# First block and second row of x issued from other queues, and the opening's VectorE order changed, in a fused Fourier-mixing and gated-MLP layer

## The chip, the cores and the metric

The kernel runs on one core of one Trainium2 chip. The metric is the device time of one execution in microseconds (us). Before the change the median of three runs is 931.79 us (931.69 to 931.9). One further execution was recorded by the hardware profiler: it took 932.1 us, of which the traced span of the core is 930.0 us.

The engines are TensorE (PE for matmuls, PEld for its weight loads), VectorE (DVE), ScalarE (ACT), GpSimd (POOL) and SyncE (SP). SyncE does nothing here but issue DMAs; ScalarE can issue DMAs too, from its own instruction stream.

## The reference

The layer has an input x of 2048 rows of 512 numbers (S = 2048, D = 512) and a condition row c that gives six modulation rows through `silu(c) @ w_mod`.

```
h = layernorm(x) * (1 + ca) + sa
a, b = h @ dft_hid_re.T, h @ dft_hid_im.T
y = dft_seq_re @ a - dft_seq_im @ b          # 2048 x 2048 matrices
x = x + ga * y
h = layernorm(x) * (1 + cb) + sb
z = gelu(h @ w_in);  z1, z2 = halves of z;  z2 = layernorm(z2)
out = x + gb * ((z1 * (w_sp @ z2 + b_sp)) @ w_out)
```

Everything is float32. A product is computed as three matmuls of rounded parts: a number is split into a high part (rounded to the matmul's format) and a low part (the rest), and high times high, high times low and low times high are added.

## The kernel before, in words

The first stage multiplies the transposed sequence matrices with the normalised rows of x. It goes in steps n = 0, 1, 2, ...; step n takes one group of 128 rows of x, numbered s = n at the start, and one 128x512 tile of the sequence matrix. `mm_a(n)` issues the step's matmuls on TensorE. From step 4 on a step is 12 matmuls (four column blocks by three products, L97 to L99), in the order high x high, high x low, low x high inside each column block. Steps 1 to 3 are also 12 matmuls each (L576), but in three groups of four: first high of x with high of the matrix (`hh`, `ah`), then `hh` with the low part `al`, then the low part of x, `hl`, with `ah`. Step 0 is different: it multiplies the unsplit tiles in float32 (L570), so that it needs no split.

What a step needs is made by the other engines:

- The matrix arrives in blocks of 512x512, loaded by SyncE into a tile `stage` (two buffers). A block serves four steps, k = 0 to 3. For the first blocks `load_pairs` (L168) loads it in two halves, h = 0 and h = 1, each in four parts of 128 KB (32 partitions each); half 0 serves k = 0 and 1, half 1 serves k = 2 and 3. `turn_dft` transposes one tile on VectorE (L174 where k < 2, L177 else). `prep_hi(n)` does this transposition into `t` and then has ScalarE make the high part `ah` (L289). `prep_lo(n)` makes the low part `al` on VectorE (L307).
- x's rows come by `load_x`: "row" 0 and "row" 1 of the first group of four (64 KB parts, four each, L453), then rows 2 and 3 in one DMA of 512 KB (L448). `stats_first(s)` makes mean and variance of one such row on VectorE (three instructions: L467, L472, L473) and hands them to GpSimd, which makes the factors (L474, L475). `whole_first(0)` normalises row 0 on ScalarE (L484). `hi_first(s)` makes the high part `hh` straight from x on ScalarE (L510, and a one-column instruction L512), `norm_x(s)` the normalised row `xn` on ScalarE (L121), and `lo_h(s)` the low part `hl` = `xn` - `hh` on VectorE (L552). `split_first(0)` and `rest_first(0)` make row 0's two parts for later use, on ScalarE (L494) and GpSimd (L498).

The order on each engine is the order in which these calls are written: the opening, step by step by hand, stands at the end of the listing, and after it the loop over n calls `prep(n)` (which is `prep_hi(n + 3)` and `prep_lo(n + 2)`, where not yet done), `mm_a(n)` and further work that is bound to n. An engine works through its own list in order; an instruction that waits holds up all behind it on the same engine. The program gives its DMAs eight completion semaphores in turn: a DMA that takes up a semaphore is not issued before the DMA that had it last has landed, so that at most eight are under way. Before the opening, `keep_busy` runs three matmuls on a constant tile (L389).

The first DMAs of the program are issued by SyncE and ScalarE together: `two` names the issuing engine of each of four parts. ScalarE's first own work, an activation-table load for the silu function, stands behind its DMA issues (L1121).

Of the kernel before, what the change touches and what calls it, by code (L numbers as in the profile page):

```python
# [20 lines left out]
def fnet_gmlp_kernel(  # L21
# [32 lines left out]
    nc = tc.nc  # L54
# [81 lines left out]
    src, SRC_G = [], []  # L136
# [14 lines left out]
    stage, T, AH, AL = {}, {}, {}, {}  # L151
# [12 lines left out]
    def load_pairs(tile_, a, h, engs=(nc.sync,) * 4, bs=slice(0, 16)):  # L164

        v = a.rearrange("(b j) (h a s) -> h a j b s", j=32, a=4, h=2)
        for q in range(4):
            engs[q].dma_start(tile_[32 * q:32 * q + 32, bs, 64 * h:64 * h + 64], v[h, q][:, bs, :])  # L168

    def turn_dft(n, block, k, bs=slice(0, 16)):  # L170

        t = T[n].rearrange("p (b i) -> p b i", i=32)
        if SRC_G[n // 4] or k < 2:
            nc.vector.transpose(t[:, bs, :], block[:, bs, 32 * k:32 * k + 32])  # L174
        else:
            v = block.rearrange("p b (h i c) -> p b h i c", h=2, c=2)
            nc.vector.transpose(t[:, bs, :], v[:, bs, 1, :, k - 2])  # L177
# [3 lines left out]
    def load(b):  # L181
        if b < len(src):
            stage[b] = blocks.tile([P, 16, P], F32, tag="stage", bufs=2, name=f"stage{b}")
            if SRC_G[b]:
                load_block(stage[b], src[b])
            else:
                for h in range(2):
                    load_pairs(stage[b], src[b], h)
        elif b < len(src) + 2:
            j = b - len(src)  # L190
            XB.append(blocks.tile([P, 4, Q], F32, tag="stage", bufs=2, name=f"xb{j}"))
            for g in range(2):
                nc.sync.dma_start(XB[j][:, 2 * g:2 * g + 2], ht_d[g].rearrange("(k p) t -> p k t", p=P)[:, 2 * j:2 * j + 2])
                for kk in range(2):
                    TT[2 * j + kk, g] = XB[j][:, 2 * g + kk]
        elif 4 * (b - NB0) < NE - N4:
            i, gh = divmod(b - NB0, NQ)
            g, h = divmod(gh, 2)
            p = PROD[i]
            stage[b] = blocks.tile([P, 2, 16, 64], F32, tag="stage", bufs=2, name=f"stage{b}")  # L200
            for r in range(2):
                load_half(stage[b][:, r], s_d[S_OF[p], r, g] if p in S_OF else
                          quad(w_sp, r + (2 if p == 4 else 0), g + (2 if p == 1 else 0)), h)
# [5 lines left out]
    def squares(dst, block, k):  # L209
        nc.vector.transpose(dst.rearrange("p (b i) -> p b i", i=32), block[:, :, 32 * k:32 * k + 32])  # L210
# [10 lines left out]
    def slot(i, name, dtype=F32):  # L221
        return slots[0].tile([P, Q], dtype, tag=f"slot{i}", bufs=1, name=name)
# [19 lines left out]
    def form_t(n):  # L242

        if n < N1:
            gg, p, kk = (n - N2) // 4, (n - N2) // 2 % 2, n % 2
            return TT[2 * p + kk, gg]
        p = YPROD[(n - N1) // 4 % len(YPROD)]
        gg, kk = divmod(n % 4, 2)
        a, b, c, d = TT[kk, gg], TT[2 + kk, gg], TT[kk, 2 + gg], TT[2 + kk, 2 + gg]
        return {6: S2[gg, kk], 7: a if n < N3 else c, 4: b if n < N3 else d, 5: c if n < N3 else a, 3: d if n < N3 else b}[p]  # L250
# [21 lines left out]
    def prep_hi(n):  # L272
        if n >= NE or n in highs:
            return
        highs.add(n)
        if N2 <= n < N4:
            T[n] = form_t(n)
        else:
            b, k = divmod(n, 4) if n < N2 else (NB0 + (n - N4) // 4, (n - N4) % 4)
            if b != NB0:  # L280
                T[n] = blocks.tile([P, Q], F32, tag="t", bufs=2, name=f"t{n}")
            if b == NB0:
                assert n in T
            elif n >= N4:
                squares(T[n], stage[b][:, k % 2], k // 2)
            else:
                turn_dft(n, stage[b], k)
        AH[n] = SE[2][:, n - N4] if N4 <= n < N4 + 4 else blocks.tile([P, Q], F32R, tag="ah", bufs=4, name=f"ah{n}")
        nc.scalar.activation(AH[n], T[n], AF.Copy)  # L289
        if not N2 <= n < N4 and k == 3:  # L290
            stage.pop(b)
            if b != NB0:
                load(b + 2)


    def prep_lo(n):
        if n >= NE or n in lows:
            return
        lows.add(n)
        if N2 <= n < N4 and n % 4 == 3:  # L300
            AL[n] = slot(0, f"al{n}", F32R) if slots else zrow[0].tile([P, Q], F32R, tag="z1u", bufs=6, name=f"al{n}")
        elif N4 <= n < N4 + 4:
            AL[n] = slot(9 + n - N4, f"al{n}", F32R)
        else:
            AL[n] = blocks.tile([P, Q], F32R, tag="al", bufs=3, name=f"al{n}")
        t = T.pop(n)
        nc.vector.tensor_tensor(AL[n], t, AH[n].bitcast(F32), op=ALU.subtract)  # L307
# [134 lines left out]
    def load_x(g, ks=range(4), engs=(nc.sync,) * 4):  # L442

        if g not in XG:
            XG[g] = spool.tile([P, 4, D], F32, tag="x", bufs=2, name=f"x{g}")
        k0, k1 = ks[0], ks[-1] + 1
        if not g and k0 == 2:
            nc.sync.dma_start(XG[g][:, 2:, :], x[2 * P:Q, :].rearrange("(p k) d -> p k d", k=2))  # L448
        else:
            v = (x.rearrange("(g a k i) d -> g a i k d", g=NQ, a=4, i=32)[g] if g else  # L450
                 x[:2 * P, :].rearrange("(a k i) d -> a i k d", a=4, i=32))
            for a in range(4):
                engs[a].dma_start(XG[g][32 * a:32 * a + 32, k0:k1, :], v[a][:, k0:k1, :])  # L453
        for k in ks:
            X[4 * g + k] = XG[g][:, k, :]
# [4 lines left out]
    def stats_first(s):  # L460

        sums_first(s)
        norm_first(s)

    def sums_first(s):
        M1[s] = spool.tile([P, 12], F32, tag="first", bufs=4, name=f"first{s}")
        nc.vector.bn_stats(M1[s][:, :6], X[s])  # L467

    def norm_first(s):

        mv = M1[s][:, 8:]
        nc.vector.bn_aggr(mv[:, :2], M1[s][:, :6])  # L472
        nc.vector.tensor_scalar(mv[:, 1:2], mv[:, 1:2], EPS, None, op0=ALU.add)  # L473
        nc.gpsimd.tensor_tensor(mv[:, 2:3], mv[:, 1:2], mhalf, op=ALU.pow)  # L474
        nc.gpsimd.tensor_scalar(mv[:, 3:4], mv[:, 0:1], mv[:, 2:3], -1.0, op0=ALU.mult, op1=ALU.mult)  # L475
        NRM[s] = mv[:, 2:3], mv[:, 3:4]
# [22 lines left out]

    def turn_whole(n):  # L500
        T[n] = blocks.tile([P, Q], F32, tag="t", bufs=2, name=f"t{n}")
        for bs in PARTS:
            turn_dft(n, stage[0], n, bs)
        highs.add(n)
        lows.add(n)

    def hi_first(s):
        h_hi[s] = hpool.tile([P, ND, P], F32R, name=f"hh{s}")
        h = h_hi[s].rearrange("p k (a i) -> p k a i", i=32)
        nc.scalar.activation(h, X[s].rearrange("p (a k i) -> p k a i", a=4, i=32), AF.Identity,  # L510
                             bias=NRM[s][1], scale=NRM[s][0])
        nc.scalar.activation(h_hi[s][:, 0, :1], ones[:, :1], AF.Copy)  # L512
# [16 lines left out]
    def ones_x(s):  # L529
        LN[s] = spool.tile([P, D], F32, tag="xn", bufs=4, name=f"xn{s}")  # L530
        nc.gpsimd.memset(LN[s][:, 0:1], 1.0)

    def norm_x(s):

        if s not in LN:
            ones_x(s)
        elif s > 3:
            nc.gpsimd.memset(LN[s][:, 0:1], 1.0)
        apply(LN[s][:, 1:], X.pop(s)[:, 1:], NRM.pop(s))
# [9 lines left out]
    def lo_h(s):  # L549
        h_lo[s] = hpool.tile([P, ND, P], F32R, name=f"hl{s}")  # L550
        lo, h = parts_h(s, h_lo)
        nc.vector.tensor_tensor(lo, h, parts_h(s, h_hi)[0].bitcast(F32), op=ALU.subtract)  # L552
        LN.pop(s)
# [557 lines left out]
            mm([n])  # L1111


    PARTS = (slice(0, 16),)
    two = (nc.sync, nc.sync, nc.scalar, nc.scalar)
    load_x(0, range(1), two)
    stage[0] = blocks.tile([P, 16, P], F32, tag="stage", bufs=2, name="stage0")
    for bs in PARTS:
        load_pairs(stage[0], src[0], 0, two, bs)
    load_x(0, range(1, 2), two)  # L1120
    nc.scalar.activation(sc, ones[:, :ND], AF.Silu)  # L1121
    load_x(0, range(2, 4))
    load_pairs(stage[0], src[0], 1)
# [9 lines left out]
    stats_first(1)  # L1133
    prep_hi(1)
    hi_first(1)
    prep_lo(1)
    stats_first(2)
    norm_x(1)
    stats_first(3)
    hi_first(2)  # L1140
    lo_h(1)
    prep_hi(2)
    norm_x(2)
    prep_hi(3)
    prep_lo(2)
    lo_h(2)
    hi_first(3)
    norm_x(3)
    prep_lo(3)
    split_first(0)  # L1150
# [36 lines left out]
    for j, turn, weigh, row, fold, hi in ((0, (25, 26, 27, 28), (29, 29, 30, 30), 26, (34, 34, 35, 36), (40, 37, 38, 39)),  # L1187
# [8 lines left out]
        n = weigh[3] + 1  # L1196
# [20 lines left out]
    for t in range(NQ):  # L1217
        n = 8 * NQ * (t + 1)
# [136 lines left out]
    for i, p in enumerate(PROD):  # L1355
        for k in range(8):
            n = NB[p] + 2 * k
# [11 lines left out]
    for f in range(NF):  # L1369
        n = N4 + 24 + 8 * f  # L1370
# [109 lines left out]
```

## Time and profile before

| | before |
|---|---|
| median of 3 runs | 931.79 us |
| the profiled execution | 932.1 us |
| its span | 930.0 us |
| PE busy | 923.3 us, 99% of the span, 4053 matmuls |
| DVE busy | 737.4 us, 79%, 1217 instructions |
| ACT busy | 409.0 us, 44% |
| POOL busy | 198.9 us, 21% |
| chain that ended last | PE 98%, DVE 1%, DMA 0%, ACT 0% |
| DMA | 157.88 MB, mean 170 GB/s |

"Busy" is the time in which an engine worked on instructions; "chain that ended last" follows the work back from the last instruction, at each step to what released it. In the timeline a row gives the start in us from the span's start, the time that it took in us, the engine (SPq and ACTq are DMA issues from SyncE's and ScalarE's instruction streams), the line of the kernel, the operation, out<-in with shapes, and how often it was merged (x2); in square brackets, where there is one, the idle time of the engine before it and what ended that.

### The profile page before, as it was taken

The numbers are of one execution on the slowest core, as the hardware profiler recorded it, in microseconds if no ns is written. First come the engines' busy times: TensorE is split into PE (matmuls) and PEld (weight loads), VectorE is DVE, ScalarE is ACT, GpSimd is POOL, SyncE is SP. The second block draws the span as 40 slices with busy tenths as digits, with TensorE's granted clock in tenths as the row PEclk, the third lists the DMA queues.
The fourth block names the chain that finished last, engine by engine and source line by source line (L and its number), as shares of the span: only waits on it lengthen the run. The fifth ranks groups of instructions, "written<-read, shape, count | busy, mean of one in ns | idle before, by whom it ended". The sixth has DMA issues, their size and how long they took to land.

```text
span 930.0 us, 12378 instructions
## 1 busy us (share of the span) xinstructions
PE 923.3 (99%) x4053; PEld 760.2 (82%) x4053; DVE 737.4 (79%) x1217; ACT 409.0 (44%) x734; POOL 198.9 (21%) x376
## 2 busy tenths in 40 slices
PE   8999999999999999999999999999999999999998
PEld 5888888888888888888888888888888888888887
DVE  6799968787687677875678788899799789886762
ACT  5694424232132222322577877674544544331121
POOL 2330000224554165323512321331000000000000
PEclk9999999999999999999999999999999999999999
DMA  9995762757539987996463764444464555744651
GB/s 222 225 226 116 142 158 46 193 148 173 156 88 294 281 255 215 276 341 229 140 217 131 277 201 103 123 102 104 104 146 103 130 141 140 176 102 149 184 179 57
DMA packets 261584, 157.88 MB, mean 170 GB/s; under 512 B 169456, under 2 KB 229104, under 8 KB 261392
## 3 DMA queue, kind: packets, MB, share of 16 engines
q1 hardware_dynamic: 247856, 119.58, 52.2%
q0 software_dynamic: 12272, 36.86, 11.4%
q10 hardware_dynamic: 1392, 0.66, 0.2%
q8 instruction: 32, 0.52, 0.2%
q14 instruction: 32, 0.26, 0.1%
HBM read 120.33 MB, written 36.71 MB: 169 GB/s over the span
## 4 chain that ended last, share of the span: by engine, by line
PE 98%; DVE 1%; DMA 0%; ACTq 0%; ACT 0%; issue 0%; DVEq 0%
PE gp L98 12%; PE gp L97 12%; PE gp L99 12%; PE gw L99 10%; PE gw L98 10%; PE gw L97 10%; PE yp L98 3%; PE yp L97 3%; PE yp L99 3%; PE op L98 3%; PE op L99 3%; PE op L97 3%; PE fp L98 1%; PE fp L97 1%; PE fp L99 1%; PE z2s L99 1%
## 5 line engine op out<-in xcount | busy, mean ns | idle before, releaser
L289 ACT ACTIVATE ah<-t 128x512 fp32r<-128x512 f32 x235 | 148.5, 632 | 363.3 <-DVE t L174 157.8
L307 DVE TENSOR_TENSOR al<-t,ah 128x512 fp32r<-128x512 f32 x235 | 160.4, 682 | 55.2 <-PE gp L98 31.4
L98 PE MATMUL gp<-al,hh 128*128 128x512 f32 x496 | 193.2, 390 | 0.0
L97 PE MATMUL gp<-ah,hh 128*128 128x512 f32 x496 | 193.2, 389 | 0.0
L99 PE MATMUL gp<-ah,hl 128*128 128x512 f32 x496 | 193.2, 389 | 0.0
L98 PE MATMUL gw<-al,bh 128*128 128x512 f32 x400 | 155.8, 389 | 0.0
L99 PE MATMUL gw<-ah,bl 128*128 128x512 f32 x384 | 149.7, 390 | 0.0
L97 PE MATMUL gw<-ah,bh 128*128 128x512 f32 x384 | 149.6, 389 | 0.0
L97 PEld LDWEIGHTS gp<-ah,hh 128*128 128x128 f32 x496 | 93.1, 188 | 19.5
L98 PEld LDWEIGHTS gp<-al,hh 128*128 128x128 f32 x496 | 93.1, 188 | 19.5 <-DVE al L307 0.2
L99 PEld LDWEIGHTS gp<-ah,hl 128*128 128x128 f32 x496 | 93.1, 188 | 19.2
L98 PEld LDWEIGHTS gw<-al,bh 128*128 128x128 f32 x400 | 75.1, 188 | 15.7
L97 PEld LDWEIGHTS gw<-ah,bh 128*128 128x128 f32 x384 | 72.1, 188 | 15.1
L99 PEld LDWEIGHTS gw<-ah,bl 128*128 128x128 f32 x384 | 72.1, 188 | 15.1 <-DVE bl L975 0.3
L174 DVE STREAM_TRANSPOSE t<-stage 128x512 f32<-128x512 f32 x112 | 78.2, 699 | 5.7 <-DMA stage<-in_A_dft_seq_re_dram 3.7
L210 DVE STREAM_TRANSPOSE t<-stage 128x512 f32<-128x512 f32 x108 | 76.2, 706 | 2.5 <-DMA stage<-in_B_w_sp_dram 1.5
L947 POOL DMA_DIRECT2D s_d<-sj x64 | 35.1, 548 | 112.1 <-DVE sj L939 86.5
L97 PE MATMUL yp<-hth,gh 128*128 128x512 f32 x128 | 49.9, 389 | 0.0
L98 PE MATMUL yp<-htl,gh 128*128 128x512 f32 x128 | 49.8, 389 | 0.0
L99 PE MATMUL yp<-hth,gl 128*128 128x512 f32 x128 | 49.8, 389 | 0.0
L692 POOL DMA_DIRECT2D ht_d<-hturn x62 | 40.9, 665 | 21.2 <-DVE hturn L688 17.4
L97 PE MATMUL op<-woh,uh 128*128 128x512 f32 x110 | 42.8, 390 | 0.0
(248 smaller groups left out, 1502.6 us busy)
## 6 DMA issues: line engine op xcount, KB each, us to landing
sj<-in_B_w_sp_dram SPq DMA_DIRECT2D x32, 512.0 KB, 7.1
s_d<-sj POOLq DMA_DIRECT2D x64, 256.0 KB, 4.4
stage<-s_d SPq DMA_DIRECT2D x128, 128.0 KB, 2.8
stage<-in_A_dft_seq_re_dram SPq DMA_DIRECT2D x48, 256.0 KB, 5.4
stage<-in_A_dft_seq_im_dram SPq DMA_DIRECT2D x48, 256.0 KB, 5.5
stage<-in_B_w_sp_dram SPq DMA_DIRECT2D x88, 128.0 KB, 3.2
stage<-in_A_dft_seq_im_dram SPq DMA_DIRECT2D x32, 128.0 KB, 3.7
wm<-in_w_mod_dram SPq DMA_DIRECT2D x16, 256.0 KB, 5.4
```

The source lines that it names most:

```text
L97: nc.tensor.matmul(acc, ah, bh, start=first, stop=False, skip_group_check=go_on)
L98: nc.tensor.matmul(acc, ah, bl, start=False, stop=False, skip_group_check=go_on)
L99: nc.tensor.matmul(acc, al, bh, start=False, stop=last, skip_group_check=go_on)
L174: nc.vector.transpose(t[:, bs, :], block[:, bs, 32 * k:32 * k + 32])
L210: nc.vector.transpose(dst.rearrange("p (b i) -> p b i", i=32), block[:, :, 32 * k:32 * k + 32])
L289: nc.scalar.activation(AH[n], T[n], AF.Copy)
L307: nc.vector.tensor_tensor(AL[n], t, AH[n].bitcast(F32), op=ALU.subtract)
L692: eng.dma_start(v[a, i], ht[32 * a:32 * a + 32].rearrange("c (b r) -> c b r", r=32))
L947: nc.gpsimd.dma_start(s_d[m, r, g][b * P:(b + 1) * P, :], a)
```

## The change

Three edits, all in the opening.

The loads: of the four parts of the first half block, three instead of two are issued by SyncE, and one instead of two by ScalarE. All four parts of x's row 1 are issued by SyncE, where two were issued by ScalarE. The order in which the DMAs are written stays: row 0, half 0 of block 0, row 1, rows 2 and 3, half 1 of block 0.

VectorE's order: the statistics of row 2 stand ahead of `al` of step 1 instead of behind it; `hl` of row 1 stands behind the transposition of step 2 and ahead of the statistics of row 3 (it stood behind these, and ahead of the transposition); the statistics of row 3 stand behind `hl` of row 1; `al` of step 2 stands ahead of the transposition of step 3. The order of ScalarE's and GpSimd's computing stays as it is.

The list `PARTS`, which had one slice over the whole tile, goes; the same instruction is made without it.

```diff
     def turn_whole(n):
         T[n] = blocks.tile([P, Q], F32, tag="t", bufs=2, name=f"t{n}")
-        for bs in PARTS:
-            turn_dft(n, stage[0], n, bs)
+        turn_dft(n, stage[0], n)
         highs.add(n)
...
-    PARTS = (slice(0, 16),)
     two = (nc.sync, nc.sync, nc.scalar, nc.scalar)
     load_x(0, range(1), two)
     stage[0] = blocks.tile([P, 16, P], F32, tag="stage", bufs=2, name="stage0")
-    for bs in PARTS:
-        load_pairs(stage[0], src[0], 0, two, bs)
-    load_x(0, range(1, 2), two)
+    load_pairs(stage[0], src[0], 0, (nc.sync, nc.sync, nc.sync, nc.scalar))
+    load_x(0, range(1, 2))
     nc.scalar.activation(sc, ones[:, :ND], AF.Silu)
     load_x(0, range(2, 4))
     load_pairs(stage[0], src[0], 1)
@@ -1133,18 +1130,18 @@
     stats_first(1)
     prep_hi(1)
     hi_first(1)
+    stats_first(2)
     prep_lo(1)
-    stats_first(2)
     norm_x(1)
+    hi_first(2)
+    prep_hi(2)
+    lo_h(1)
     stats_first(3)
-    hi_first(2)
-    lo_h(1)
-    prep_hi(2)
     norm_x(2)
+    prep_lo(2)
     prep_hi(3)
-    prep_lo(2)
+    hi_first(3)
     lo_h(2)
-    hi_first(3)
     norm_x(3)
     prep_lo(3)
     split_first(0)
```

## Rows read from the trace of the kernel before

**Rows 1.** Busy time by stretch: from:to, us, then PE, PEld, DVE, ACT, POOL busy (instructions).

```profile
7.06:14.15 7.09, 6.71 (x20) 3.62 (x20) 6.07 (x15) 4.14 (x9) 2.84 (x6) 1.00 1.09 255
...
19.73:60.00 40.27, 40.27 (x179) 33.30 (x178) 34.39 (x61) 28.05 (x57) 13.79 (x44) 1.00 1.19 225
60.00:920.00 860.00, 860.00 (x3794) 711.69 (x3793) 688.67 (x1129) 369.01 (x657) 179.54 (x314) 1.00 0.61 167
```

**Rows 2.** Chain that ended last, 0 to 20 us: start, us, what.

```profile
2.12 3.92 DMA stage<-in_A_dft_seq_re_dram
6.24 0.70 DVE t L174
...
14.15 5.73 PE gp L576 x24
```

**Rows 3.** Timeline of the first 30 us: DMA issues of SyncE.

```profile
1.65 0.95 SPq L168 DMA_DIRECT2D stage<-in_A_dft_seq_re_dram  x2
...
2.95 0.78 SPq L453 DMA_DIRECT2D x<-in_A_x_dram  x2
...
5.20 0.35 SPq L448 DMA_DIRECT2D x<-in_A_x_dram  x1
...
5.60 2.02 SPq L168 DMA_DIRECT2D stage<-in_A_dft_seq_re_dram  x4
```

**Rows 4.** Waits of SyncE, 0 to 40 us: total, times, longest.

```profile
SPq L448 <- DMA stage<-in_A_dft_seq_re_dram: 1.4, 1, 1.4
```

**Rows 5.** DMA issues at 7.1 to 7.2 us: count, size, us to landing.

```profile
stage<-in_A_dft_seq_re_dram SPq DMA_DIRECT2D x1, 128.0 KB, 4.1
```

**Rows 6.** DMA issues at 5.1 to 5.3 us.

```profile
x<-in_A_x_dram SPq DMA_DIRECT2D x1, 512.0 KB, 3.9
```

**Rows 7.** DMA issues at 2.9 to 3.0 us.

```profile
x<-in_A_x_dram SPq DMA_DIRECT2D x1, 64.0 KB, 3.3
```

**Rows 8.** DMA packets, both queues at work, 3.6 to 5.4 us.

```profile
DMA packets 1668, 0.48 MB, mean 265 GB/s; under 512 B 1631, under 2 KB 1631, under 8 KB 1668
```

**Rows 9.** DMA packets, SyncE's queue alone, 8.4 to 9.8 us.

```profile
DMA packets 1598, 0.40 MB, mean 284 GB/s; under 512 B 1598, under 2 KB 1598, under 8 KB 1598
```

**Rows 10.** Timeline of the first 30 us: VectorE.

```profile
9.49 0.69 DVE L307 TENSOR_TENSOR al<-t,ah 128x512 fp32r<-128x512 f32 x1 [0.70 <-ACT ah L289]
...
10.10 0.69 DVE L467 BATCH_NORM_STATS2 first<-x 128x6 f32<-128x512 f32 x1
...
11.11 0.69 DVE L467 BATCH_NORM_STATS2 first<-x 128x6 f32<-128x512 f32 x1
...
12.12 0.69 DVE L552 TENSOR_TENSOR hl<-xn,hh 128x512 fp32r<-128x512 f32 x1
...
12.73 1.30 DVE L177 STREAM_TRANSPOSE t<-stage 128x512 f32<-128x512 f32 x2
...
14.13 0.69 DVE L307 TENSOR_TENSOR al<-t,ah 128x512 fp32r<-128x512 f32 x1
...
17.08 0.69 DVE L552 TENSOR_TENSOR hl<-xn,hh 128x512 fp32r<-128x512 f32 x1 [0.87 <-ACT xn L121]
...
19.09 0.69 DVE L307 TENSOR_TENSOR al<-t,ah 128x512 fp32r<-128x512 f32 x1
```

**Rows 11.** Timeline of the first 30 us: ScalarE.

```profile
5.93 1.09 ACT L484 ACTIVATE xn<-x,first 128x256 f32<-128x256 f32 x2 [0.47 <-POOL first L475]
...
14.71 0.62 ACT L289 ACTIVATE ah<-t 128x512 fp32r<-128x512 f32 x1
...
16.18 0.80 ACT L121 ACTIVATE xn<-x,first 128x511 f32<-128x511 f32 x1
```

**Rows 12.** Timeline of the first 30 us: TensorE, weight loads and matmuls.

```profile
12.87 1.20 PE L576 MATMUL gp<-ah,hl 128*128 128x512 f32 x4 [0.26 <-DVE hl L552]
...
19.84 0.19 PEld L98 LDWEIGHTS gp<-al,hh 128*128 128x128 f32 x1
...
19.96 0.39 PE L98 MATMUL gp<-al,hh 128*128 128x512 f32 x1
```

## The prediction

> **What bounds the kernel now.** I began with the page's shares (PE busy 99% of the span), so the only time to be had is where TensorE stands still. Busy time by stretch shows where: from 19.73 us to 60 and from 60 to 920 the PE is busy for the whole stretch, to the hundredth [rows 1]. Whatever happens in the opening, the end therefore moves by as much as TensorE's place in its own list moves once it has run into that closed stretch, and by nothing else. The second view is the chain of waits of the first 20 us. It goes from the DMA of the first half block, issued by ScalarE at 2.12 and landed at 6.04, to the first transposition at 6.24 (0.20 after the landing), and by VectorE and ScalarE to matmuls that run without a break from 14.15 on [rows 2]. From 7.06 to 14.15 the PE was busy for 6.71 of 7.09 us [rows 1]; its one stated wait there is 0.26 for `hl` of row 1, ahead of the matmuls at 12.87 [rows 12].
>
> The third view, the engines' timelines, shows a point that the chain hides, since it had no idle time: step 4. Its second product needs `al`, which VectorE began at 19.09 and had after 0.69, at 19.78 [rows 10]; the weight load that goes with it is at 19.84 and its matmul at 19.96 [rows 12]. So `al` of step 4 came just in time, with no slack. An earlier PE before it gains nothing unless this `al` is earlier too, and if this `al` is later, the end is later. So I follow the change to that point.
>
> **The chain to that `al`, before.** ScalarE makes `ah` of step 3 at 14.71, then `hh` of row 3, then `xn` of row 3 at 16.18, which is done at 16.98 [rows 11]. VectorE has idled 0.87 for it and starts `hl` of row 3 at 17.08; two transpositions follow, then `ah` of step 4, then `al` at 19.09 [rows 10]. From `ah` of step 3 to this `al` are 19.09 - 14.71 = 4.38 us. None of these instructions is moved among its neighbours, so I carry the 4.38 over. What moves is the transposition of step 3, on which `ah` of step 3 waits: it is the second of the pair at 12.73 and ends at 14.03 [rows 10].
>
> **VectorE's new order.** The steps from instruction to instruction, from the same rows: a statistics group 1.01 (10.10 to 11.11 to 12.12), a subtraction 0.61 (9.49 to 10.10; 12.12 to 12.73), a transposition 0.60 (two take 1.30, one alone 0.70 [rows 2, 10]).
>
> - Statistics of row 2, now first. VectorE is free at 9.49 - 0.70 = 8.79 and idled until 9.49 for `ah` of step 1 [rows 10]. The edit puts 1.01 of work into this hole. But rows 2 and 3 of x, issued at 5.20 with 3.9 to landing, come at 9.1 [rows 3, 6]; 0.20 later, at 9.3, the statistics can begin. So the hole is not filled, it is kept for 0.5. `al` of step 1 starts at 9.3 + 1.0 = 10.3 and is done at 11.0. Behind this wait are queued `al` and the transposition of step 2, and TensorE's second group of step 1 waits for the former; that group starts near 11.5 (the third group at 12.87, less its wait of 0.26, less 1.1 for four matmuls, of which the third group shows 1.20 [rows 12]), so 11.0 is in time by about 0.4.
> - The transposition of step 2, now ahead of `hl` and of the statistics of row 3. VectorE is free for it at 10.3 + 0.6 = 10.9. It needs the second half of block 0, in four parts issued from 5.60 to 7.62 [rows 3]; the last goes out at about 7.13 and lands 4.1 later, at 11.2 [rows 5]. So it starts at 11.4, where it started at 12.73. In the order of before this landing was hidden by 1.5 us; now it decides.
> - From there: `hl` of row 1 at 12.0 (12.12 before), statistics of row 3 at 12.6, `al` of step 2 at 13.65, transposition of step 3 at 14.25, done at 14.95. Before, that was done at 14.03. Between the two transpositions now stand a statistics group and two subtractions, 2.2 us, where nothing stood.
> - `ah` of step 3 can start at about 15.0. Before, it was at 14.71, because ScalarE was still at `xn` of row 2, so only 0.3 of the 0.9 counts. ScalarE idles more than a microsecond ahead of it.
> - `al` of step 4: 15.0 + 4.38 = 19.4, done at 20.1. TensorE's matmul with it comes at 20.25 instead of 19.96: **+0.3**.
>
> **What TensorE gains, and loses again.** `ah` of step 2 follows a transposition that ends at 12.1, so step 2 no longer waits for it: `hl` of row 1 is done at 12.7, the third group of step 1 runs from 12.8 to 13.8, and step 2 starts there instead of at 14.15 (the 14.15 of [rows 2]). The 0.3 of gain is kept through steps 2 and 3 and ends at step 4 as a longer wait for `al` (0.3 + 0.3). Sum: 0 from the gain, +0.3 from `al`.
>
> **The queues.** SyncE issues at 0.47 each for parts of the block (0.95 for two) and 0.4 for parts of a row [rows 3]. Its list gets one part of the block and two of row 1 more: 0.47 + 0.8 = 1.3 us. These go into the 1.4 us in which it stood before the load of rows 2 and 3 and waited for a landing of the first half block [rows 4]; it is free at about 4.95 and that load still goes at 5.20. If the cover were gone by the landing being earlier, the load would go out up to 0.25 sooner, which helps. The cost of having three parts in one queue is not in the trace: from both sides, the half block lands between 0.3 sooner (no part of row 1 runs beside its last part in the other queue) and 0.5 later (the third part goes out 0.5 later). Row 1's last part goes out near 4.55 where it went at 3.5; by the 3.3 that a part of it took [rows 7] it lands at 7.85 at worst, at about 6.9 if bytes moved set it; I take the latter, since the bytes ahead of it are the same. Neither end reaches the sum: row 1's statistics at 8.0 would put the transposition of step 1 at 9.0, ahead of the 9.3 above, and step 2's transposition still waits for 11.2. At the first matmul nothing is gained either: it waits for row 0 normalised at 5.93, which itself stood 0.47 for GpSimd's factors [rows 11], so that ScalarE's freedom from three DMA issues stays idle.
>
> The Trainium skill ("DMA: Bandwidth & Descriptors", section "Issuing engines are not separate DMA queues") says that DMAs from either issuing engine run on the same 16 DMA engines, and that issuing from several saves only the issue time. The trace agrees: one queue alone moved 284 GB/s [rows 9], both together 265 [rows 8]. By this rule the change gives up 1.3 us of ScalarE's issue time and no bandwidth, which speaks against the change, and against the rival below in which the landings slip by more than that.
>
> Profile against median: the profiled execution took 932.1 with a span of 930.0, so 2.1 lies outside the span and stays; it is 0.3 over the median of 931.79. The sum is 932.1 + 0.3 = 932.4 on its own terms, which is **932.1** against the median.
>
> **The rivals.**
> 1. *The landings come sooner.* If the second half lands before 10.7, the statistics of row 2 decide and step 2's transposition starts at 10.9: all of the chain is 0.5 sooner than I have it, the end at 932.1 - 0.5 = 931.6; if rows 2 and 3 too are there at 8.8, another 0.5, 931.1. For it: SyncE could issue 0.25 sooner. Against it: that brings 11.2 to 10.95 alone, and the step-4 `al` to just where it was.
> 2. *SyncE's list backs up* (the other side). The load of rows 2 and 3 takes up a semaphore of the first half block; if that is its part behind two others in one queue, or one of row 1's, it is issued not at 5.20 but between 5.9 and 6.9, and the second half with it: landing at 11.9 to 12.9, the `al` of step 4 0.7 to 1.7 later still, 932.8 to 933.8. It makes the kernel measurably slower from a landing at 12.8 on. For it: the 1.4 us wait [rows 4] shows that a landing gates this load. Against it: ScalarE's part is now alone in its queue and first out.
> 3. *The edits do not reach TensorE*: the early wait goes, `al` of step 4 stays just in time because another instruction than the one I follow sets it. 931.8.
>
> **How the numbers follow.** Forecast 0.60 (931.8 to 932.5), rival 1 0.22, rival 2 0.10, rival 3 0.08. Range: 931.2 takes in the most of rival 1, 932.8 the milder half of rival 2. A run of this kernel tells 0.2%, 1.9 us, from no change. All idle time that TensorE has from 7.06 to the closed stretch is under half a microsecond, so rival 1 can't reach 929.9: faster 0.01. Slower needs rival 2's far end, 0.04. Same 0.95.
>
> **What would show it.** In the timeline after: statistics of row 2 starting about 9.3, behind a wait on x's DMA; the transposition of step 2 at 11.4 behind a wait on the block's DMA; ScalarE idle ahead of `ah` of step 3 at about 15.0; an idle PE of about 0.6 at step 4's L98, ended by `al` L307. Wrong if no such wait stands at step 4, if the load of rows 2 and 3 moves from 5.2 by over 0.3, or if TensorE's first gapless matmul after step 4 comes before 19.9.

## The result, and the profile after

The changed kernel takes 934.0 us (median of 12 runs, 933.6 to 935.43) where the kernel before takes 932.01 on the same chips (12 runs, 931.69 to 932.78): a ratio of 1.0022, 95% interval 1.0013 to 1.0031. It is 2.0 us slower; the forecast was 932.1 with a range from 931.2 to 932.8. The profiled execution took 933.6, span 931.5 against 930.0, and is the fastest of the twelve, so the two traces show 1.5 of the 2.0 us.

Busy time by stretch (columns as in [rows 1]) shows that the loss lies ahead of 22 us: behind that TensorE is as closed as before.

```profile
7.06:14.15 7.09, 6.39 (x19) 3.59 (x20) 5.35 (x12) 3.71 (x8) 2.01 (x4) 1.00 0.95 234
19.73:60.00 40.27, 40.05 (x176) 32.61 (x175) 33.91 (x59) 28.05 (x56) 12.88 (x41) 1.00 1.19 223
60.00:920.00 860.00, 860.00 (x3794) 711.62 (x3793) 690.27 (x1132) 370.43 (x659) 180.84 (x318) 1.00 0.62 167
```

TensorE lost 0.32 us more between 7.06 and 14.15 (6.39 busy, 6.71 in [rows 1]), and 0.22 behind 19.73. Its matmuls and the waits of its weight loads name the places (first the timeline, then the waits from 0 to 40 us: total, times, longest):

```profile
20.31 0.50 PE L97 MATMUL gp<-ah,hh 128*128 128x512 f32 x1
21.03 0.50 PE L98 MATMUL gp<-al,hh 128*128 128x512 f32 x1 [0.22 <-DVE al L307]
```

```profile
PEld gp L575 <- ACT hh L509: 1.5, 1, 1.5
...
PEld gp L98 <- DVE al L307: 0.5, 1, 0.5
...
PEld gp L97 <- ACT ah L289: 0.4, 1, 0.4
```

The second wait is the forecast one: step 4's L98 for `al`. (The busy time understates it: L98 starts 0.72 behind L97 here, 0.23 before, and for 0.50 of that L97 counts as busy.) But the matmul comes at 21.03, not at the 20.25 of the prediction (19.96 in [rows 12]). The first wait was not forecast: step 1 waits for `hh` of row 1. It does not set the end: the third line shows that at step 4 the weight load of L97, ahead of L98, stood 0.4 for `ah` as well. The last VectorE instruction, which waits for the last matmul, then starts 1.17 later (927.60 against 926.43 in the chain of waits of each); that is the opening's loss, carried through. The other 0.3 of the span lies behind the last matmul.

VectorE's timeline shows the 0.8 us beyond the forecast.

```profile
8.38 0.69 DVE L467 BATCH_NORM_STATS2 first<-x 128x6 f32<-128x512 f32 x1 [1.52 <-DMA x<-in_A_x_dram]
...
9.40 0.70 DVE L174 STREAM_TRANSPOSE t<-stage 128x512 f32<-128x512 f32 x1
...
10.30 0.69 DVE L467 BATCH_NORM_STATS2 first<-x 128x6 f32<-128x512 f32 x1 [0.20 <-DMA x<-in_A_x_dram]
...
11.31 0.68 DVE L307 TENSOR_TENSOR al<-t,ah 128x512 fp32r<-128x512 f32 x1
...
12.03 0.71 DVE L177 STREAM_TRANSPOSE t<-stage 128x512 f32<-128x512 f32 x1
12.66 0.65 DVE L551 TENSOR_TENSOR hl<-xn,hh 128x512 fp32r<-128x512 f32 x1
13.23 0.68 DVE L467 BATCH_NORM_STATS2 first<-x 128x6 f32<-128x512 f32 x1
...
14.41 0.69 DVE L307 TENSOR_TENSOR al<-t,ah 128x512 fp32r<-128x512 f32 x1
15.02 0.70 DVE L177 STREAM_TRANSPOSE t<-stage 128x512 f32<-128x512 f32 x1
...
18.27 0.69 DVE L551 TENSOR_TENSOR hl<-xn,hh 128x512 fp32r<-128x512 f32 x1 [1.15 <-ACT xn L121]
...
20.29 0.69 DVE L307 TENSOR_TENSOR al<-t,ah 128x512 fp32r<-128x512 f32 x1
```

The statistics of row 1 wait 1.52 us for x and start at 8.38, and every step behind them is late: the statistics of row 2 at 10.30 (forecast 9.3), the transposition of step 2 at 12.03 (11.4), that of step 3 at 15.02 (14.25), `al` of step 4 at 20.29 (19.4; 19.09 in [rows 10]). Three landings are behind this, and the timeline does not part them: row 1's, that of rows 2 and 3 (0.20 of wait), and that of the second half block, which the transposition of step 2 needs. On ScalarE the hole ahead of `ah` of step 3 is there:

```profile
5.88 1.09 ACT L484 ACTIVATE xn<-x,first 128x256 f32<-128x256 f32 x2 [2.26 <-DMA x<-in_A_x_dram]
...
15.76 0.64 ACT L289 ACTIVATE ah<-t 128x512 fp32r<-128x512 f32 x1 [0.68 <-DVE t L177]
```

SyncE's issues, against [rows 3], went as forecast: the load of rows 2 and 3 goes out at 5.09, even a little sooner than 5.20.

```profile
1.64 1.48 SPq L168 DMA_DIRECT2D stage<-in_A_dft_seq_re_dram  x3
...
3.16 1.89 SPq L453 DMA_DIRECT2D x<-in_A_x_dram  x4
...
5.09 0.42 SPq L448 DMA_DIRECT2D x<-in_A_x_dram  x1
5.56 2.39 SPq L168 DMA_DIRECT2D stage<-in_A_dft_seq_re_dram  x4
```

What went otherwise is the landing. The DMA issues at 4.6 to 4.7 us (row 1's last part), at 5.0 to 5.2 (rows 2 and 3) and at 7.05 to 7.1 (the last part of the second half block), the last column us to landing:

```profile
x<-in_A_x_dram SPq DMA_DIRECT2D x1, 64.0 KB, 3.6
```

```profile
x<-in_A_x_dram SPq DMA_DIRECT2D x1, 512.0 KB, 5.2
```

```profile
stage<-in_A_dft_seq_re_dram SPq DMA_DIRECT2D x1, 128.0 KB, 4.8
```

Row 1 is complete at 4.62 + 3.6 = 8.3 instead of 6.9, rows 2 and 3 at 10.3, where [rows 6] had 3.9 to landing and 9.1, and the second half block at 7.09 + 4.8 = 11.9, where [rows 5] had 4.1 and the prediction 11.2. A DMA here gives sixteen completion marks (steps of its semaphore) and is complete with the last. Of row 1's last part eight were in by 6.82, fifteen by 7.62, and the last came at 8.26; of rows 2 and 3 eight by 8.59 (8.47 before), fifteen by 9.29, the last at 10.27; of the block's last part fifteen by 11.08 (11.03 before), the last at 11.90 (11.28). So a few marks come late, not the transfer as a whole.

### The profile page after: what moved, and what is told of

It is laid out like the page before. It is cut to its first block, busy times and chain, and to the rows that moved or that the text cites. A ratio compares the mean times of both kernels' runs of the same rounds, so it can differ in the third digit from the quotient of the medians.

```text
span 931.5 us, 12379 instructions
## 1 busy us (share of the span) xinstructions
PE 925.1 (99%) x4053; PEld 760.2 (82%) x4053; DVE 737.7 (79%) x1217; ACT 409.3 (44%) x734; POOL 199.9 (21%) x376
## 4 chain that ended last, share of the span: by engine, by line
PE 97%; SPq 1%; DMA 0%; DVE 0%; issue 0%; ACT 0%; DVEq 0%
PE gp L98 12%; PE gp L99 12%; PE gp L97 12%; PE gw L98 10%; PE gw L99 10%; PE gw L97 10%; PE yp L99 3%; PE yp L97 3%; PE yp L98 3%; PE op L98 3%; PE op L97 3%; PE op L99 3%; PE fp L98 1%; PE fp L99 1%; PE fp L97 1%; PE z2s L99 1%
## 5 line engine op out<-in xcount | busy, mean ns | idle before, releaser
L98 PE MATMUL gp<-al,hh 128*128 128x512 f32 x496 | 193.1, 389 | 0.2 <-DVE al L307 0.2
L97 PE MATMUL gp<-ah,hh 128*128 128x512 f32 x496 | 193.1, 389 | 0.0
L98 PE MATMUL gw<-al,bh 128*128 128x512 f32 x400 | 155.6, 389 | 0.0
L97 PE MATMUL gw<-ah,bh 128*128 128x512 f32 x384 | 149.4, 389 | 0.0
L98 PEld LDWEIGHTS gp<-al,hh 128*128 128x128 f32 x496 | 93.1, 188 | 19.9 <-DVE al L307 0.7
L97 PEld LDWEIGHTS gp<-ah,hh 128*128 128x128 f32 x496 | 93.1, 188 | 19.7 <-ACT ah L289 0.4
L99 PEld LDWEIGHTS gp<-ah,hl 128*128 128x128 f32 x496 | 93.1, 188 | 19.4
L98 PEld LDWEIGHTS gw<-al,bh 128*128 128x128 f32 x400 | 75.1, 188 | 15.5
L97 PEld LDWEIGHTS gw<-ah,bh 128*128 128x128 f32 x384 | 72.1, 188 | 15.1
L97 PE MATMUL yp<-hth,gh 128*128 128x512 f32 x128 | 49.8, 389 | 0.0
L98 PE MATMUL yp<-htl,gh 128*128 128x512 f32 x128 | 49.8, 389 | 0.0
L97 PE MATMUL op<-woh,uh 128*128 128x512 f32 x110 | 42.8, 389 | 0.0
```

The costliest lines, as they stand in the source:

```text
L97: nc.tensor.matmul(acc, ah, bh, start=first, stop=False, skip_group_check=go_on)
L98: nc.tensor.matmul(acc, ah, bl, start=False, stop=False, skip_group_check=go_on)
L99: nc.tensor.matmul(acc, al, bh, start=False, stop=last, skip_group_check=go_on)
```

## The experiments

The theory to begin with was that the loads carry the loss; its rival, the prediction's own view, that VectorE's order does. All times stand beside runs of the kernel before on the same chip. "Row 1", "rows 2, 3" and "half 1" (the second half block) are the last completion marks, "turn 2" is the start of the transposition of step 2, "PE" is the shift of the last matmul against the first profile of before. These columns come from one execution each, e1 to e4, e5 to e8, e9 to e12 and e13 to e16 on four chips; how far a landing scatters is the question of e13.

| kernel | row 1 | rows 2, 3 | half 1 | turn 2 | PE | median us | before | ratio, 95% interval |
|---|---|---|---|---|---|---|---|---|
| before, first profile | 6.88 | 9.06 | 11.28 | 12.73 | 0 | | | |
| changed | 8.26 | 10.27 | 11.90 | 12.03 | +1.17 | 934.0 | 932.01 | 1.0022 (1.0013 to 1.0031) |
| e1 queues only | 8.32 | 10.69 | 12.01 | 14.10 | +1.36 | 933.66 | 932.04 | 1.0017 (1.0008 to 1.0026) |
| e2 order only | 6.77 | 9.32 | 11.32 | 11.40 | +0.44 | 932.54 | 932.04 | 1.0004 (0.9995 to 1.0013) |
| e3 row 1 on two queues | 7.00 | 10.21 | 11.86 | 11.97 | +1.14 | 933.99 | 932.04 | 1.0017 (1.0008 to 1.0025) |
| e4 block on two queues | 6.73 | 9.37 | 11.65 | 11.73 | +0.81 | 933.23 | 932.04 | 1.0012 (1.0003 to 1.0021) |
| e5 all on SyncE | 8.19 | 12.21 | 13.82 | 13.97 | +3.11 | 935.31 | 932.22 | 1.0029 (1.0018 to 1.0039) |
| e6 three parts on ScalarE | 7.07 | 11.14 | 12.63 | 12.90 | +2.07 | 934.06 | 932.22 | 1.0018 (1.0009 to 1.0026) |
| e7 rows 2, 3 by ScalarE | 9.59 | 8.12 | 12.39 | 13.05 | +3.14 | 935.63 | 932.22 | 1.0035 (1.0023 to 1.0048) |
| e8 statistics of row 2 first | 6.56 | 10.12 | 11.49 | 13.39 | +0.63 | 932.64 | 932.22 | 1.0004 (0.9995 to 1.0013) |
| e9 changed, rows 2, 3 in two | 7.44 | 9.25, 10.35 | 11.94 | 12.12 | +1.22 | 933.22 | 932.04 | 1.0011 (1.0002 to 1.0020) |
| e10 before, rows 2, 3 in two | 6.61 | 7.81, 9.20 | 10.98 | 12.52 | -0.16 | 931.83 | 932.04 | 0.9996 (0.9987 to 1.0005) |
| e11 changed, rows 2, 3 last | 6.94 | 13.20 | 9.48 | 14.84 | +4.77 | 937.67 | 932.04 | 1.0060 (1.0048 to 1.0073) |
| e12 before, in two, statistics first | 6.76 | 7.83, 8.53 | 11.12 | 11.79 | -0.88 | 931.20 | 932.04 | 0.9990 (0.9981 to 0.9999) |
| e13 before again | 6.67 | 10.92 | 12.17 | 13.59 | +0.84 | 933.03 | 932.4 | one run |
| e14 changed again | 8.09 | 9.88 | 11.81 | 11.89 | +0.85 | 933.28 | 932.4 | one run |
| e15 order only, in two | 6.84 | 7.88, 9.96 | 11.55 | 11.73 | +0.66 | 932.61 | 932.4 | 1.0003 (0.9994 to 1.0012) |
| e16 changed, rows 2, 3 in four | 7.40 | 9.83 | 12.27 | 12.39 | +1.43 | 932.98 | 932.4 | 1.0011 (1.0002 to 1.0020) |

The columns "half 1" and "turn 2" carry the answer. In ten of the twelve traces of VectorE's new order (all but e7 and e11) the transposition of step 2 starts 0.08 to 0.27 behind the landing of the second half block, and step 4's L98 follows it by 8.8 to 9.1 us (8.85 forecast). In six of the ten VectorE waits for the block, by 0.28 to 1.40 us; in the other four (changed, e3, e5, e6) it comes free only then, behind rows 2 and 3. In the six traces of the old order, with e8's edit or without, turn 2 starts 0.67 to 2.1 behind the landing and does not wait for it.

**The two halves of the change.** e1 is the kernel before with the changed loads, e2 the changed kernel with the loads of before:

```diff
 # e1
-    for bs in PARTS:
-        load_pairs(stage[0], src[0], 0, two, bs)
-    load_x(0, range(1, 2), two)
+    load_pairs(stage[0], src[0], 0, (nc.sync, nc.sync, nc.sync, nc.scalar))
+    load_x(0, range(1, 2))
 # e2
-    load_pairs(stage[0], src[0], 0, (nc.sync, nc.sync, nc.sync, nc.scalar))
-    load_x(0, range(1, 2))
+    load_pairs(stage[0], src[0], 0, two)
+    load_x(0, range(1, 2), two)
```

> Only the loads are changed (three parts of the first half block and all of row 1 on SyncE's queue); VectorE's order is that of before. Theory Q (the loads: row 1's last part, fourth in a row on one queue, lands near 8.3 us instead of 6.9): statistics of row 1 start near 8.4 instead of 7.07 and everything behind them is 1.3 later, so the run is 1.2 to 2.0 us over before, about the whole loss of the changed kernel. Rival V (VectorE's new order carries the loss, as the prediction had it, by the transposition of step 2 that waits for the second half block): within 0.3 us of before.

> Only VectorE's order is changed; the loads go out from SyncE and ScalarE in turns as before. Theory Q: row 1 lands at 6.9 and its statistics start at 7.1; then the prediction's chain holds: the transposition of step 2 waits for the second half block until about 11.4, al of step 4 starts near 19.4, 0 to 0.4 us over before. Rival V: 1.2 to 2.0 us over before.

e1 loses 1.6 us: the loads carry most of the loss. It does so by a path of its own, though: under the old order VectorE waits for row 1, every step behind is as much later, and the second half block, there at 12.01, is not waited for (turn 2 at 14.10). VectorE's wait for row 1 in e1:

```profile
8.45 0.69 DVE L467 BATCH_NORM_STATS2 first<-x 128x6 f32<-128x512 f32 x1 [1.48 <-DMA x<-in_A_x_dram]
```

In e2 the prediction's chain stands as it was written (statistics of row 2, transpositions of steps 2 and 3; then step 4's matmul):

```profile
9.35 0.69 DVE L467 BATCH_NORM_STATS2 first<-x 128x6 f32<-128x512 f32 x1 [0.67 <-DMA x<-in_A_x_dram]
...
11.40 0.71 DVE L177 STREAM_TRANSPOSE t<-stage 128x512 f32<-128x512 f32 x1 [0.36 <-DMA stage<-in_A_dft_seq_re_dram]
...
14.21 0.71 DVE L177 STREAM_TRANSPOSE t<-stage 128x512 f32<-128x512 f32 x1
```

```profile
20.28 0.50 PE L98 MATMUL gp<-al,hh 128*128 128x512 f32 x1 [0.23 <-DVE al L307]
```

Forecast for these four were 9.3, 11.4, 14.25 and 20.25. So with the loads of before, whose second half block landed at 11.32, the prediction's chain is right step by step. The time, 0.5 over before, can't be told from none by its interval.

**Which of the loads.** e3 and e4 take back one of the two edits to the loads each:

```diff
 # e3
-    load_x(0, range(1, 2))
+    load_x(0, range(1, 2), two)
 # e4
-    load_pairs(stage[0], src[0], 0, (nc.sync, nc.sync, nc.sync, nc.scalar))
+    load_pairs(stage[0], src[0], 0, two)
```

> The changed kernel with row 1's four parts on two queues again (two on SyncE, two on ScalarE); three of the first half block's parts stay on SyncE. Theory Q in the form that row 1's four issues in one queue are to blame: row 1 lands by 7.0, time within 0.4 us of before. If instead the third block part on SyncE's queue is to blame: row 1 lands near 8.3 and the time is that of the changed kernel, 1.2 to 2.0 us over before.

> The changed kernel with the first half block two and two on the queues as before; all of row 1 stays on SyncE. Theory Q in the form that row 1's four issues in one queue are to blame: row 1's last part lands at 7.5 to 8.3 and the time is 0.6 to 2.0 us over before. If the third block part is to blame: within 0.4 us of before.

Neither answer came out clean. e3 has row 1 back at 7.0, as the theory said, but rows 2 and 3 land at 10.21 and the second half block at 11.86; turn 2 starts at 11.97 and `al` of step 4 at 20.22 (20.29 in the changed kernel), and it loses 1.9 all the same. So row 1's landing is not what the changed kernel's loss hangs on. e4 has row 1 at 6.73 although all four parts are on SyncE; there its last part goes out 0.72 ahead of rows 2 and 3 (4.19 and 4.91), in the changed kernel 0.47 (4.62 and 5.09). So neither the count of row 1's issues on one queue nor the block's third part is the cause by itself; the suspicion fell on the load of rows 2 and 3.

**Depth of a queue.** e5 puts everything on SyncE, e6 three block parts on ScalarE, e7 has ScalarE issue rows 2 and 3; e8 is the kernel before with one edit of the order.

```diff
 # e5
-    load_x(0, range(1), two)
+    load_x(0, range(1))
-    load_pairs(stage[0], src[0], 0, (nc.sync, nc.sync, nc.sync, nc.scalar))
+    load_pairs(stage[0], src[0], 0)
 # e6
-    load_pairs(stage[0], src[0], 0, (nc.sync, nc.sync, nc.sync, nc.scalar))
+    load_pairs(stage[0], src[0], 0, (nc.sync, nc.scalar, nc.scalar, nc.scalar))
 # e7, in load_x
-            nc.sync.dma_start(XG[g][:, 2:, :], ...
+            nc.scalar.dma_start(XG[g][:, 2:, :], ...
 # e8, against before
-    prep_lo(1)
     stats_first(2)
+    prep_lo(1)
```

> The changed kernel with row 0 and the whole first half block on SyncE's queue as well; ScalarE issues none. Theory D (the more of the first transfers stand in SyncE's one queue, the later the slowest of the 16 DMA engines finishes what stands behind them: row 1 and rows 2 and 3): rows 2 and 3 land at 10.3 or later, the time is 2.0 to 3.5 us over before. Rival B (only the split of the block's parts between two queues matters, three against one, not the depth): in one queue nothing is uneven, rows 2 and 3 land near 9.5, time within 1.2 us of before apart from row 0, whose parts go out 0.9 later and hold the first matmul up by as much.

> The changed kernel with the first half block one part on SyncE and three on ScalarE; row 1 stays on SyncE. Theory D: SyncE's queue is two parts shorter than in the changed kernel, so row 1 lands by 6.9 and rows 2 and 3 by 9.4, while the last part of the block may land 0.3 to 0.6 later on ScalarE's queue: 0.2 to 1.0 us over before. Rival B (three against one hurts on either queue): 1.2 to 2.0 us over before.

> The changed kernel with rows 2 and 3 issued by ScalarE instead of SyncE, behind its table load and the silu. Theory D: that load no longer stands behind three block parts and row 1 in one queue, so it lands near 9.1 instead of 10.3 and the statistics of row 2 start near 9.4 unless row 1 is still late (8.3): 0.5 to 1.3 us over before. Rival B or a slow DMA engine whatever the queue: rows 2 and 3 at 10.2 or later, 1.2 to 2.0 us over before.

> The kernel before with one edit alone: statistics of row 2 ahead of al of step 1; the loads, and the order of the rest, stay. If the prediction's chain is right (what moves is the transposition of step 3 and with it ah of step 3): statistics of row 2 at 9.3, al of step 1 at 10.3, statistics of row 3 at 10.9, the pair of transpositions at 12.5 instead of 12.73, al of step 4 at 18.9 instead of 19.09: 0.1 to 0.2 us under before, too little for the timed runs to tell, but visible in the trace at step 4's second matmul. If the wait for rows 2 and 3 eats it: equal or up to 0.3 over.

e5 came out as theory D said, but e6 speaks against it, as far as one execution can: with SyncE's queue two parts shorter, rows 2 and 3 were later still (11.14). In e5, too, row 1's last part goes out 0.47 ahead of the large load on the same queue (6.08 and 6.56), and it lands after 2.1 us. e7 missed both expectations: ScalarE's queue was free, so the 512 KB went out at 2.19, ahead of block parts that were not yet through, and the first half block itself landed only at 8.85. e8 is the important one. Its loads are those of before, row by row, and yet rows 2 and 3 landed at 10.12. So a late landing needs neither a deep queue nor the changed loads, and the question became whether the load of rows 2 and 3 makes its own late marks.

In e6 and e7 a second thing shows, in the stretches of TensorE (PE busy, then the granted clock): in e6 it stood still from 5.97 to 8.09, and behind that ran for a while at the lower of its two levels, 1.2 GHz; in e7 the granted clock was 0.50 from 9.7 to 12.0, behind 3.22 us of standing still.

```profile
5.90:8.00 2.10, 0.07 (x1) 1.00 1.02 248
8.00:10.50 2.50, 2.41 (x3) 0.55 1.04 207
```

**The large load.** e9 and e10 load rows 2 and 3 by two DMAs of 256 KB, in the changed kernel and in that of before; e11 moves the 512 KB load behind the second half block; e12 is e10 with e8's edit.

```diff
 # e9, e10, e12, in load_x
-            nc.sync.dma_start(XG[g][:, 2:, :], x[2 * P:Q, :].rearrange("(p k) d -> p k d", k=2))
+            for k in ks:
+                nc.sync.dma_start(XG[g][:, k, :], x[2 * P:Q, :].rearrange("(p k) d -> p k d", k=2)[:, k - 2, :])
 # e11
-    load_x(0, range(2, 4))
     load_pairs(stage[0], src[0], 1)
+    load_x(0, range(2, 4))
```

> The changed kernel with rows 2 and 3 of x loaded by two DMAs of 256 KB (2 KB packets) instead of one of 512 KB (4 KB packets). Theory S (the one large load makes one DMA engine fall 1 to 2 us behind near 6 us, and row 1's last part, which now goes out 1 us later, is caught by that): row 1 lands by 7.2, row 2 by 8.5, 0 to 0.6 us over before. Rival D (one queue's depth, whatever the packet size): row 1 near 8.3, 1.2 to 2.0 us over before.

> The kernel before with rows 2 and 3 of x loaded by two DMAs of 256 KB. VectorE reaches the statistics of row 2 only at 10.1, so an earlier landing gains nothing by itself: equal to before within 0.3 us. Theory S: the second half of the first block, queued behind, lands without the late engine, by 11.1. Rival D: it lands at 11.3 or later.

> The changed kernel with the 512 KB load of rows 2 and 3 issued behind the second half of block 0 instead of ahead of it. Theory S: with the large load gone from 6 us, row 1 lands by 7.1 (against 8.26); rows 2 and 3 land only at 11.5 to 12.5, so the statistics of row 2 are late and the time is 1.5 to 3.0 us over before for that reason. Rival D: row 1 lands near 8.3 all the same.

> The kernel before with rows 2 and 3 in two DMAs and the statistics of row 2 ahead of al of step 1: both changes that the traces so far favour. If row 2 lands by 8.5, its statistics fill VectorE's idle 0.7 at 8.8, everything behind is 0.4 to 0.6 earlier, al of step 4 at 18.5 to 18.7 instead of 19.09: 0.3 to 0.6 us under before. If row 2 lands later than 9.3: equal or over.

e11 is the most direct test of what stands behind row 1, in one trace. Row 1's last part goes out at 4.63, as in the changed kernel (4.62), on the same queue behind the same parts; only what comes behind it differs. Its issue at 4.6 to 4.7, and that of rows 2 and 3 at 7.1 to 7.2:

```profile
x<-in_A_x_dram SPq DMA_DIRECT2D x1, 64.0 KB, 2.3
```

```profile
x<-in_A_x_dram SPq DMA_DIRECT2D x1, 512.0 KB, 6.0
```

2.3 us to landing instead of 3.6, complete at 6.94 instead of 8.26; the late marks have moved with the 512 KB load, which now takes 6.0. By e5, a large load directly behind is not the whole condition. (Its late landing costs e11 5.6 us, more than expected, part of it at the lower clock: 0.50 granted from 17 to 19 us.) In e9 row 1 is nearly cured (7.44) and row 2 is there when VectorE comes to it, but the last mark of its 256 KB load, too, is late (9.25 where half the marks were in by 7.66), and e9 keeps 1.2 of the loss. Its trace shows why: the second half block is as late as in the changed kernel, and VectorE waits for it.

```profile
12.12 0.71 DVE L177 STREAM_TRANSPOSE t<-stage 128x512 f32<-128x512 f32 x1 [1.15 <-DMA stage<-in_A_dft_seq_re_dram]
...
20.25 0.69 DVE L307 TENSOR_TENSOR al<-t,ah 128x512 fp32r<-128x512 f32 x1
```

e10 is level with before. e12 beats both kernels, the one before by 0.84 us (0.0010, interval 0.0001 to 0.0019, so only just clear of none), and its trace shows by what: the statistics of row 2 no longer wait, and fill the hole of 0.70 in [rows 10]; `al` of step 4 is 0.93 sooner.

```profile
8.59 0.65 DVE L468 BATCH_NORM_STATS2 first<-x 128x6 f32<-128x512 f32 x1
...
18.16 0.69 DVE L307 TENSOR_TENSOR al<-t,ah 128x512 fp32r<-128x512 f32 x1
```

**Scatter, and four parts.** e13 and e14 are the kernels before and after, unchanged, profiled again. e15 is e2 with rows 2 and 3 in two DMAs, e16 the changed kernel with them in four:

```diff
 # e16, in load_x
-            nc.sync.dma_start(XG[g][:, 2:, :], x[2 * P:Q, :].rearrange("(p k) d -> p k d", k=2))
+            v = x[2 * P:Q, :].rearrange("(a i k) d -> a i k d", a=4, k=2)
+            for a in range(4):
+                nc.sync.dma_start(XG[g][32 * a:32 * a + 32, 2:, :], v[a])
```

> The kernel before, profiled once more, to see how far its landings scatter. Theory U (an uneven split of the first block between the two queues is what makes one DMA engine fall far behind): rows 2 and 3 land at 9.0 to 9.4, as in the first profile. Rival R (the slow engine comes and goes with any split; even splits showed 9.06, 9.32, 9.37 and 10.12 so far): about as likely over 9.7.

> The changed kernel, profiled once more. Theory U: row 1 at 7.7 or later, rows 2 and 3 at 10.0 or later, as in its first profile (8.26 and 10.27) and with its loads under the old order (8.32 and 10.69). Rival R: one of both back at 7.0 and 9.3.

> VectorE's new order on the loads of before, with rows 2 and 3 in two DMAs. If the order lost 0.5 only by waiting for rows 2 and 3: statistics of row 2 start at 8.6, and the time is that of the best version so far, 0.6 to 1.0 us under before. If, as the prediction has it, the transposition of step 2 still waits for the second half block (11.0 to 11.2) and the transposition of step 3 stands 2.8 behind it: al of step 4 at 19.1 to 19.3, 0 to 0.3 us over before.

> The changed kernel with rows 2 and 3 in four DMAs of 128 KB (4 KB packets as in the single one). Theory S (one load of 512 KB in one DMA makes the engine fall behind): row 1 by 7.3, rows 2 and 3 by 9.3, 0.2 to 0.8 us over before. If packets of 4 KB do it, or the uneven split (theory U): row 1 near 8, rows 2 and 3 over 10, 1.2 to 2.0 us over before.

e13 settles the question of scatter, against theory U: the kernel before, issue at 4.78, has the load of rows 2 and 3 take 6.1 us, and VectorE wait for it.

```profile
x<-in_A_x_dram SPq DMA_DIRECT2D x1, 512.0 KB, 6.1
```

```profile
10.95 0.69 DVE L467 BATCH_NORM_STATS2 first<-x 128x6 f32<-128x512 f32 x1 [0.98 <-DMA x<-in_A_x_dram]
```

That execution took 933.03, against 932.1 for the first profile. So the 9.1 that the prediction took from one profile was at the good end of what the two profiles of this kernel show, 9.06 and 10.92; the second half block's landing moved with it, from 11.28 to 12.17. e14 repeats the changed kernel's pattern: row 1 at 8.09. It also parts the three landings: rows 2 and 3 are there at 9.88 before VectorE comes to them at 9.91, and what VectorE waits for last is the second half block.

```profile
9.91 0.69 DVE L467 BATCH_NORM_STATS2 first<-x 128x6 f32<-128x512 f32 x1
...
11.89 0.71 DVE L177 STREAM_TRANSPOSE t<-stage 128x512 f32<-128x512 f32 x1 [0.28 <-DMA stage<-in_A_dft_seq_re_dram]
```

In e16 the four loads of 128 KB, same bytes and same packets of 4 KB, have no mark so late: at 5.2 to 6.7, four issues, a median of 3.0 to landing, in each the last mark within 0.2 of the fifteenth.

```profile
x<-in_A_x_dram SPq DMA_DIRECT2D x4, 128.0 KB, 3.0
```

They take four issues of SyncE's time instead of one, land as a whole at 9.83, and the second half block behind them lands later still (12.27); 0.6 of the loss stays. e15 shows that the order's part of the loss is not the wait for row 2: that is gone (its statistics start at 8.67), and still the transposition of step 2 starts at 11.73, at the second half block, and `al` of step 4 at 19.81.

## Why the prediction was wrong

- *The path.* Right: everything came by `al` of step 4 at L98, with a wait of 0.5 there, and TensorE was closed behind it. From `ah` of step 3 to this `al` were 20.29 - 15.76 = 4.53 (4.38 carried over), and between the two moved transpositions 2.99 (2.85). e3, with row 1 in time, and e2, with the loads of before, show the same chain.
- *The price of the order.* Right: +0.3 forecast, +0.32 at L98 in e2. e15 confirms the reason: the wait for the second half block.
- *SyncE's list.* Right: the added issues fitted into its wait, and ScalarE's freedom changed nothing at the first matmul.
- *The step that failed* is in the paragraph on the queues, which carries the landings of the kernel before over to new loads: "Neither end reaches the sum", since "step 2's transposition still waits for 11.2". That this transposition waits for the second half block and decides was right; the 11.2 was not. The block was complete at 11.90, and at 11.81 in e14, because its last part took 4.8 and 4.7 us to land where 4.1 was carried over. The transposition started at 12.03 (11.89) instead of 11.4. Of the 0.78 by which L98 missed its 20.25 this is 0.63; the other 0.15 is the way from there to L98, 9.00 for 8.85.
- *Row 1 and rows 2 and 3* were mis-sized in the same way, but neither was needed for the miss. Row 1's last part was to land "at 7.85 at worst, at about 6.9 if bytes moved set it"; it landed at 8.26, and 8.09 the second time. By the steps of the trace (statistics of row 2 at 10.0, `al` of step 1 at 11.05) that alone puts the transposition of step 2 at 11.7. Rows 2 and 3 at 10.27 instead of 9.1 put it at 11.9, level with the block in this one trace; in e14 they cost nothing, and in e9 row 2 and nearly row 1 are cured and `al` of step 4 is where it was.
- *A slip in the same sentence.* The transposition of step 1 at 9.0 is not "ahead of the 9.3": it holds VectorE until 9.6, so the statistics of row 2 could not start before. With the block at 11.2 that changes nothing.
- *The landings were taken from one profile each*, for instructions that the change moves onto those very landings. In the order of before, the statistics of row 2 came at 10.10, one microsecond behind their landing, and the transposition of step 2 1.45 behind its own, and most of the scatter was hidden. None of the prediction's three signs of being wrong came up, and none of them looks at a landing.
- *Rival 2* came nearest (932.8 to 933.8). Its landing of the second half block, 11.9, came true, by luck: the loads were to be issued late; they were issued on time and landed late.
- *The rule on issuing engines* (the Trainium skill, "DMA: Bandwidth & Descriptors", "Issuing engines are not separate DMA queues": DMAs share the same DMA engines whoever issues them, and several issuers save issue time alone) does not speak of when a transfer is complete. What I drew from it, that landings could not slip, does not follow. The mean rate was not untouched either: from 2.6 to 7.6 us the core moved 227 GB/s (233 in e14, 229 in e1) with the changed loads, and 250 (271 in e13, 263 in e2, 242 in e8) with those of before; no run tells whether the queues do that.

By the medians, loads alone cost 1.6 and the order alone 0.5; together 2.1, and 2.0 was measured. That this adds up is in part luck: the traces show +1.36 (e1) and +0.44 (e2), but +1.17 and +0.85 for the changed kernel, and e1 loses by row 1 where the changed kernel loses by the second half block. Of the 2.0, 0.4 lies between the profiled execution and the median and 0.3 behind the last matmul, and no trace here says what they are.

Shown is the path: in the new order the second half block's landing sets step 4, by the waits in e14, e9, e4 and e16. That the changed loads bring it later rests on the medians (2.0 over before with them, 0.5 without, in the same order); the landings themselves, 11.81 to 12.01 in three traces with them and 11.28 to 12.17 in four without, overlap. Shown, too, is that the load of rows 2 and 3 has late marks in the kernel before as well. That it holds up row 1's last part is what e11 says, against e5. Not settled is why some marks of a large DMA come late, and by what the changed loads make it worse.

## What to carry to other kernels

Where an edit moves a consumer onto a landing, take that landing from several executions, and from its last part, and ask for every landing on the chain which one comes last; the hidden slack of the old order (1.45 us at the second half block) was worth more than the hole that the edit was to fill. A small load that is needed at once may suffer from a large one directly behind it (e11, but not e5): look at what follows it in the queue as well as at what precedes it. And a load that two consumers share can be cut along the consumers: rows 2 and 3 in two DMAs made the early statistics pay in the old order (e12), which they did not in one (e8); in the new order, where the second half block decides, the cut paid nothing that the runs could tell (e15 against e2).

## What the runs showed of the hardware

A single DMA of 512 KB over 128 partitions had its last completion mark up to 2.05 us behind the fifteenth (e13: 8.87 and 10.92; 0.40 in the first profile of before), and in e3, e5 and e11 three or four of its marks came 1.4 to 2.7 behind the eighth; four DMAs of 128 KB over 32 partitions each had the last mark 0.02 to 0.2 behind the fifteenth (e16). The lateness passes on: in e13 the last marks of the four block parts queued behind the large load were 1.2 to 1.65 behind their fifteenth. A 64 KB DMA issued 0.47 ahead of the large one took 3.5 to 3.7 us to land in three traces (changed kernel, e14, e1) and 2.3 without it (e11), but 2.1 in e5, where all loads stood in one queue. And TensorE's granted clock was 0.55 from 8.0 to 10.5 in e6, after the engine had stood still for 2.12 us; in e5, after 1.79 us, it was 1.00 over the same stretch.
